# Attention, Mish FFN and four experts on one core: a new order for the first block, and expert weights fetched earlier

## The chip, the cores and the metric

The kernel runs as one program on one core of a Trainium2 chip. The metric is the device time of one execution in microseconds (us). The kernel before takes 945.83 us, the median of three runs (945.04, 945.83 and 948.88). What a measurement of this kernel can tell from no change is about 0.5%, some 4.7 us.

## The reference

Three stages are chained. Attention has 2 batches, 8 heads, 768 positions and 64 columns per head, with a bias that falls with distance; a key is kept when it is one of the first `n_global` (8) or among the last `n_local` (96). Its result, 1536 tokens of 512 columns, goes through a dense layer pair with a Mish gate, and that through four experts with ReLU, mixed by given probabilities:

```
scores = q @ k.T / 8 + bias;  a = softmax(where(keep, scores, -1e9));  x = a @ v
h = x @ w_in                       # 512 -> 2048
g = h * tanh(log1p(exp(min(h, 20))))
y = g @ w_out                      # 2048 -> 512
out = sum over e of p[e] * (relu(y @ w1[e]) @ w2[e])     # 512 -> 1024 -> 512
```

`w_in` and `w_out` come as 64-bit floats and are read as 64-bit words; everything else is 32-bit.

## The kernel before, in words

The 1536 tokens are three blocks of 512. For each block there are 16 pairs of attention (one pair: 128 queries and two heads), 16 steps of the FFN (128 hidden columns each) and 32 steps of the experts. A step is a "hidden" product, a gate, and a "project" product into four PSUM accumulators. The change touches block 0 alone, which is written out by hand in `first_block` (L788 to L886); blocks 1 and 2 are driven by the loop in `run` and are untouched.

In block 0 the products are single fp32 matmuls: `hidden_first` (L747) has four per step and `project_first` (L757) four per step, each shown by the trace as two instructions. The weights of FFN step c, 1 MB of 64-bit words, are loaded by `fetch` (L557) into one of four buffers (`big` 0 and 1, `raw` 0 and 1; table `TURN`), and turned into fp32 by `narrow` (L570): one ScalarE instruction (L584) and three VectorE instructions (L587, L589, L591), after which SyncE stores the result to HBM (L593, `wfirst`) for block 1. The buffer is free for step c+4 when step c is converted. All these loads and stores go through SyncE's one queue, in program order.

The order of the work in block 0 is a string, `PLAN` (L42). Each letter stands for one call, and the k-th use of a letter is for pair, step or part k. An engine executes its own instructions in exactly the order in which these calls issue them, so a letter that waits holds up everything behind it on the same engine. The letters:

- attention of one pair: S scores (PE), X bias and maximum (VectorE), E exponentials (ScalarE), D inverse sums of two pairs (VectorE), N scaling of the probabilities (GpSimd, L372), T transposes (PE), C copy of the transposes (ScalarE, L382) or Z the same on VectorE, A product with v (PE), F copy of the result of four pairs on ScalarE or G on VectorE (L396)
- conversion of one FFN step's weights: a (ScalarE), then t three times (VectorE)
- FFN: H hidden product, P project product (PE); the gate is e (ScalarE), c, n (VectorE), l (two on ScalarE), u, m, v, g (VectorE)
- w: a third of the splitting of an expert's weights into two parts (one ScalarE cast L609, two VectorE subtractions L612); i, j and 1 to 6: the start of block 1's attention

At H of step 0 all 16 pairs must be through (`n["F"] == 4`), since the FFN sums over all heads. Before the change the expert weights of steps 16 to 18 are fetched at the first `w`, from inside `part` (L852 to L861):

Of the kernel before, what the change touches and what calls it, by code (L numbers as in the profile page):

```python
# [11 lines left out]
I64 = mybir.dt.int64  # L12
AF = mybir.ActivationFunctionType
ALU = mybir.AluOpType

P = 128
B, H, S, D = 2, 8, 768, 64
# [7 lines left out]
NF1 = 16  # L25
# [14 lines left out]


PLAN = (  # L42
    "SSYXXESYSEXSEDXNXESNTDCTXSENANCTXESACTDEAXNSCNETXACTDEGANCSNaAXatTTtCSCAEXtAESDGNSXNTXEStTCDSEXNACNX"
    "EAtaTDTtNCSCANXEtAEtTTCGCADatNAaNtTtCTACtaAtGtHattteHacntlteHuamcvgnPetlctauHtmvngtlPteaucmHtvngtlPt"
    "eaucmHtvgntlPteaucmtHvngtlPteaucmtHvgntltPeucmtvHngtltPeucmtvHngtltaPeucmvngHtltautiPemcvgnPtltutHmw"
    "vwgwePwcnwlwHumvgePcnlHuwmwvwgeHcnlPuemcvngHlumvPegcnlPumvgj1P23456"
)

AFTER = {
# [8 lines left out]


@with_exitstack  # L60
def fused_attention_ffn_moe(ctx: ExitStack, tc: tile.TileContext, qkv, qk, vz, q_t, k_t, v_n, nloc, nglob, wff, wts, probs, out):
    nc = tc.nc
    nc.scalar.preload_act_table_set("natural_log_exp_and_others")
    const = ctx.enter_context(tc.tile_pool(name="const", bufs=1))


    nw = const.tile([P, 2], I64, tag="nw", name="nw")
    nc.sync.dma_start(nw[:, 0:1], nloc.unsqueeze(0).broadcast_to([P, 1]))
    nc.scalar.dma_start(nw[:, 1:2], nglob.unsqueeze(0).broadcast_to([P, 1]))

    early = ExitStack()
    setup = early.enter_context(tc.tile_pool(name="setup", bufs=1))
# [58 lines left out]
    big = [const.tile([P, 2048], F32, tag=f"big{n}", name=f"big{n}") for n in range(2)]  # L131
    for n, raw in enumerate(raws):
        at = slice(P if n < 2 else 0, 3 * P)
        nc.sync.dma_start(raw[:, 0:6 * P].rearrange("p (n c) -> p n c", n=2)[:, :, at],
                          qk[2 * n:2 * n + 2, :, at].rearrange("n p c -> p n c"))
        if wff.dtype == I64 and n % 2:
            nc.sync.dma_start(big[n // 2].bitcast(I64), wff[n // 2])

    narrow = nc.values_load(flag[0:1, 0:1], min_val=0, max_val=1)
    env = dict(qkv=qkv, qk=qk, vz=vz, q_t=q_t, k_t=k_t, v_n=v_n, wff=wff, wts=wts, out=out, ident=ident, nl=nl, ng=ng,  # L140
# [181 lines left out]
class FirstPair(NarrowPair):  # L322
# [43 lines left out]
        nc.vector.tensor_scalar(r, r, 1e-9, None, ALU.add)  # L366
        nc.vector.reciprocal(r, r)

    def scale(self):
        for j in range(2):  # L370
            p = self.p[:, j, 0:self.nk * P]
            self.nc.gpsimd.tensor_scalar(p, p, self.sum[:, j:j + 1], 0.0, ALU.mult, ALU.add)  # L372

    def trans(self):
        self.pt_ps = self.body.bank(f"pt{self.u}", 0)
# [147 lines left out]
class Body:  # L523
# [33 lines left out]
    def fetch(self, s):  # L557

        kind, t, n = self.steps[s]
        if kind == "ffn" and self.wide and t == 0:  # L560
            self.w64[s] = (self.big + self.twice)[TURN[n]].bitcast(I64)
            if n > 1 or not self.loaded:
                self.nc.sync.dma_start(self.w64[s], self.wff[n])
            return
        if kind == "ffn" and self.wide and t > self.first:
            return
        self.w32[s] = self.wpool.tile([P, 1024], F32, tag="w", name=f"w{s}")
        self.nc.sync.dma_start(self.w32[s], (self.wts if kind == "moe" else self.wfirst if self.wide else self.wff)[n])
# [219 lines left out]
    def first_block(self, ready, now):  # L788


        nc = self.nc
        pairs = [FirstPair(self, k) for k in range(TB // P * NP)]
        then = Attention(self, self.pair, 1)
        n = dict.fromkeys("SXEDNTCAFHecnlumvgPatw", 0)
        narrowing = [self.narrow(c) for c in range(NF1)]
        parts = [self.part(c) for c in range(NF1, NF1 + 3)]
        self.x0 = self.xy.tile([P, KC, TB], F32, tag="xyh", name="x0")

        for pair in pairs:
            pair.load()  # L800

        def ahead():
            while ready["fetch"] < NF1:
                c = ready["fetch"]
                before = [m for m in range(c) if TURN[m] == TURN[c]][-1:]
                if n["S"] < FREE.get(TURN[c], 0) or any(n["t"] < 3 * m + 3 for m in before):
                    break
                now("fetch", c + 1)

        def scores(k):  # L810
            pairs[k].scores()
            ahead()

        def warm(k):

            nc.tensor.matmul(self.bank(f"warm{k}", 0), self.ident, self.ident.unsqueeze(1).to_broadcast([P, 4, P]), start=True, stop=True)

        def inverse(k):
            assert n["E"] >= 2 * k + 2
            pairs[2 * k].inverse()  # L820

        def scale(k):
            assert n["D"] > k // 2
            pairs[k].scale()

        def take(engine):
            def run(k):
                assert n["A"] >= 4 * k + 4
                pairs[4 * k].take(engine)
                ahead()  # L830
            return run

        def hidden(s):
            assert n["F"] == 4 and n["t"] >= 3 * s + 3
            self.accumulating = True
            self.hidden_first(s)
            ahead()

        def project(s):
            self.project_first(s)  # L840

        def begin(c):
            assert (c < 2 or n["A"] >= min(2 * c - 2, len(pairs))) and (c < 10 or n["P"] > c - 10)
            next(narrowing[c])

        def convert(k):
            c = k // 3
            assert n["a"] > c
            next(narrowing[c], None)
            ahead()  # L850

        def part(k):  # L852
            c, third = divmod(k, 3)
            assert ready["fetch"] >= NF1 and n["S"] == len(pairs) and n["P"] >= 8 + 2 * c
            if third == 0:
                now("fetch", NF1 + 3)
                next(parts[c])
            try:
                parts[c].send("vector" if third else None)
            except StopIteration:  # L860
                pass  # L861

        def begin_next(k):
            assert n["t"] >= 36
            then.load(4)

        pair = lambda stage, *args: lambda k: getattr(pairs[k], stage)(*args)
        ops = {
            "S": scores, "X": pair("biased"), "E": pair("exps"), "D": inverse, "N": scale, "T": pair("trans"),
            "C": pair("copy", nc.scalar.copy), "Z": pair("copy", nc.vector.tensor_copy), "A": pair("av"),  # L870
            "F": take(nc.scalar.copy), "G": take(nc.vector.tensor_copy), "a": begin, "t": convert, "w": part,
            "Y": warm, "H": hidden, "e": self.mish_exp, "c": self.mish_cap, "n": self.mish_n, "l": self.mish_r,
            "u": self.mish_u, "m": self.mish_m, "v": self.mish_v, "g": self.gate_first, "P": project,
            "i": begin_next, "j": lambda k: then.split(k + 1),
            "1": lambda k: then.ahead(), "2": lambda k: then.scores(), "3": lambda k: then.softmax(),
            "4": lambda k: then.norm(), "5": lambda k: then.trans(), "6": lambda k: then.av(),
        }
        same = dict(Z="C", G="F")
        for token in PLAN:
            kind = same.get(token, token)  # L880
            for other in AFTER.get(kind, ()):
                assert n[other] > n[kind], (token, n[kind], other)
            ops[token](n.setdefault(kind, 0))
            n[kind] += 1
        ready["narrow"], ready["part"] = NF1, NF1 + n["w"] // 3
        return then, n["P"]  # L886
# [163 lines left out]
```

## Time and profile before

| | us |
|---|---|
| median of three runs | 945.83 |
| lowest, highest | 945.04, 948.88 |
| the profiled execution, its own time | 944.16 |
| its span, first to last instruction | 942.3 |
| TensorE (PE) busy in the span | 910.1 (97%) |
| VectorE, ScalarE, GpSimd busy | 527.8, 440.5, 379.6 |

The profiled execution is 1.67 us below the median. TensorE is busy nearly all the time; what can be won lies in its idle 32 us and in stretches where its clock is granted at half. A position in the trace is given in us from the span's start.

### The profile page before, as it was taken

How to read it: one execution, taken by the hardware profiler on the slowest of the kernel's cores; microseconds unless marked ns; L12 is line 12 of the kernel's file. 1: busy time of each engine (PE TensorE's matmuls, PEld its weight loads, DVE VectorE, ACT ScalarE, POOL GpSimd, SP SyncE). 2: the span in 40 equal slices, each digit the busy share in tenths (PEclk: the TensorE clock that was granted, in tenths of full speed). 3: DMA queues.
4: the chain of work that ended last, by engine and by line, in shares of the span. 5: the costliest groups of instructions: out<-in, count | busy, mean ns of one | idle time of the engine just before them, and what ended most of it. 6: DMA issues, size and time to landing. Idle time of an engine off the chain costs nothing.

```text
span 942.3 us, 11540 instructions
## 1 busy us (share of the span) xinstructions
PE 910.1 (97%) x3962; PEld 697.8 (74%) x3962; DVE 527.8 (56%) x1041; ACT 440.5 (47%) x860; POOL 379.6 (40%) x391
## 2 busy tenths in 40 slices
PE   8899979999899999999999999999999999999997
PEld 4744434787678888877777888888888888888886
DVE  4889957777673178888777621228886121112122
ACT  4844324776663256556776642323445332432330
POOL 3500000577575444437666754400004454454450
PEclk7999999999999999999999999999999999999999
DMA  8876450543312478863435223044562342323301
GB/s 308 296 284 224 160 196 1 201 157 134 112 68 90 156 263 298 296 261 134 143 126 201 69 90 106 29 178 179 195 252 94 107 134 99 103 90 97 105 23 49
DMA packets 40517, 143.88 MB, mean 153 GB/s; under 512 B 4736, under 2 KB 7552, under 8 KB 38400
## 3 DMA queue, kind: packets, MB, share of 16 engines
q1 hardware_dynamic: 40160, 143.02, 42.6%
q8 instruction: 33, 0.54, 0.2%
q14 instruction: 36, 0.29, 0.1%
q10 hardware_dynamic: 288, 0.03, 0.0%
HBM read 114.71 MB, written 28.31 MB: 152 GB/s over the span
## 4 chain that ended last, share of the span: by engine, by line
PE 71%; DVE 15%; ACT 8%; issue 2%; DMA 2%; POOL 0%; SPq 0%; ACTq 0%; DVEq 0%
PE h L627 29%; PE acc L733 28%; PE acc L762 5%; PE h L750 4%; DVE kl L231 2%; ACT p L275 1%; DVE nr L672 1%; PE o L297 1%; ACT wh L609 1%; DVE e L667 1%; PE pt L192 1%; DVE nr L678 1%; DVE n L655 1%; DVE e L682 1%; DVE n L648 1%
## 5 line engine op out<-in xcount | busy, mean ns | idle before, releaser
L612 POOL TENSOR_TENSOR wl<-w,wh 128x512 fp32r<-128x512 f32 x218 | 290.2, 1352 | 324.2 <-ACT wh L609 314.6
L708 DVE SCALAR_TENSOR_TENSOR gl<-h,gh 128x512 fp32r<-128x512 f32 x96 | 66.2, 689 | 267.3 <-ACT gh L703 267.3
L609 ACT CAST wh<-w 128x1024 fp32r<-128x1024 f32 x112 | 117.7, 1050 | 121.8 <-PE acc L733 106.2
L733 PE MATMUL acc<-wh,gh 128*128 128x512 f32 (+1 forms) x384 | 151.4, 394 | 0.0
L733 PE MATMUL acc<-wh,gl 128*128 128x512 f32 (+1 forms) x384 | 148.9, 388 | 0.0
L733 PE MATMUL acc<-wl,gh 128*128 128x512 f32 (+1 forms) x384 | 148.7, 387 | 0.0
L703 ACT ACTIVATE gh<-h 128x512 fp32r<-128x512 f32 x96 | 57.3, 597 | 114.4 <-PE h L627 114.4
L733 PEld LDWEIGHTS acc<-wh,gl 128*128 128x128 f32 x384 | 72.1, 188 | 15.1
L733 PEld LDWEIGHTS acc<-wl,gh 128*128 128x128 f32 x384 | 72.2, 188 | 14.1
L733 PEld LDWEIGHTS acc<-wh,gh 128*128 128x128 f32 x384 | 72.2, 188 | 14.0
L240 POOL TENSOR_TENSOR v<-raw,v 128x256 fp32r<-128x256 f32 x32 | 26.9, 841 | 116.6 <-ACT v L239 116.6
L750 PE MATMUL h<-x,w 128*128 128x512 f32 x128 | 57.2, 593 | 0.8 <-DVE x L396 0.8
L187 POOL TENSOR_SCALAR p<-p,st 128x256 f32<-128x256 f32 (+1 forms) x64 | 29.9, 479 | 66.5 <-DVE st L185 65.6
L627 PE MATMUL h<-y0h,wh 128*128 128x512 f32 x128 | 52.6, 411 | 2.5 <-DVE st L264 1.5
L275 ACT ACTIVATE p<-t,st 128x256 f32<-128x256 f32 (+1 forms) x96 | 46.4, 486 | 17.5 <-DVE st L264 16.5
L627 PE MATMUL h<-y1h,wh 128*128 128x512 f32 x128 | 50.7, 396 | 0.1
L627 PE MATMUL h<-y0h,wl 128*128 128x512 f32 x128 | 50.5, 395 | 0.0
L627 PE MATMUL h<-y0l,wh 128*128 128x512 f32 x128 | 50.4, 394 | 0.0
L627 PE MATMUL h<-y1l,wh 128*128 128x512 f32 x128 | 49.9, 390 | 0.0
L733 PE MATMUL acc<-gh,wh 128*128 128x512 f32 x128 | 49.9, 390 | 0.0
L627 PE MATMUL h<-y1h,wl 128*128 128x512 f32 x128 | 49.9, 390 | 0.0
L627 PE MATMUL h<-y2h,wh 128*128 128x512 f32 x128 | 49.9, 390 | 0.0
(152 smaller groups left out, 1821.3 us busy)
## 6 DMA issues: line engine op xcount, KB each, us to landing
w<-in_wts SPq DMA_DIRECT2D x96, 512.0 KB, 3.5
raw<-in_qkv SPq DMA_DIRECT2D x32, 512.0 KB, 3.9
big<-in_wff SPq DMA_DIRECT2D x10, 1024.0 KB, 5.9
wfirst<-w SPq DMA_DIRECT2D x16, 512.0 KB, 3.0
w<-wfirst SPq DMA_DIRECT2D x16, 512.0 KB, 4.2
wkeep<-wh SPq DMA_DIRECT2D x16, 512.0 KB, 3.1
wkeep<-wl SPq DMA_DIRECT2D x16, 512.0 KB, 2.9
wh<-wkeep SPq DMA_DIRECT2D x16, 512.0 KB, 3.2
```

The lines of the kernel that those rows point to most:

```text
L187: nc.gpsimd.tensor_scalar(self.p[:, j, 0:self.nk * P], self.p[:, j, 0:self.nk * P], st[:, 2 + j:3 + j], 0.0, ALU.mult, ALU.add)
L231: nc.vector.tensor_tensor(self.kl, self.k, self.kh.bitcast(F32), ALU.subtract)
L240: nc.gpsimd.tensor_tensor(vv[:, :, 1:3, :], v, vv.bitcast(F32)[:, :, 0:4:3, :], ALU.subtract)
L275: nc.scalar.activation(p[:, j, 0:n], t[:, j, 0:n], AF.Exp, bias=self.least[:, j:j + 1], scale=-1.0, accum_out=self.sum[:, j:j + 1])
L609: (nc.vector.tensor_copy if copy == "vector" else nc.scalar.copy)(hi, w)
L612: getattr(nc, engine or "gpsimd").tensor_tensor(lo[:, c], w[:, c], hi.bitcast(F32)[:, c], ALU.subtract)
L627: nc.tensor.matmul(ps, a[:, c], r[:, kc, :], start=m == 0, stop=m == 3 * KC - 1)
L703: self.nc.scalar.activation(gh, self.h[s], AF.Relu)
L708: nc.vector.scalar_tensor_tensor(gl, h, 0.0, gh.bitcast(F32), ALU.max, ALU.subtract)
L733: nc.tensor.matmul(acc[:, h], a, r, start=f == 0 and m == 0, stop=f == per - 1 and m == 2)
L750: self.nc.tensor.matmul(ps, self.w32[s][:, kc * P:(kc + 1) * P], self.x0[:, kc, :], start=kc == 0, stop=kc == KC - 1)
L762: self.nc.tensor.matmul(acc, w[:, 512 + d * P:512 + (d + 1) * P], g, start=s == 0, stop=s == NF1 - 1)
```

## The change

1. `PLAN` is another string of the same length. Up to the first H the counts of letters differ so: N 16 to 10, and V 0 to 6 (a new letter: the same scaling on VectorE); C 16 to 8 and Z 0 to 8; G 4 to 0 and F 0 to 4; a 6 to 5 and t 14 to 7. Over the whole string a, t, H, P, w and the gate's letters are as many as before, so 41 of 48 t stand behind the first H, where 34 stood.
2. The expert weights of steps 16 to 18 are fetched at H of step 0, and no longer at the first `w`.
3. The 64-bit weights of FFN step 1 are loaded behind all of block 0's attention inputs; before, they were loaded ahead of them.
4. `n_local` and `n_global` come in one load of one tensor on SyncE's queue; before, in two loads, on SyncE's and ScalarE's.

```
 PLAN = (
...
-    "eaucmHtvgntlPteaucmtHvngtlPteaucmtHvngtltPeucmtvHngtltPeucmtvHngtltaPeucmvngHtltautiPemcvgnPtltutHmw"
+    "tltumtPevcgnatHlttutPemcvagnHtltuatPemcvngtHltuatPemcvgntlHtutmPetvcgntlHtutmPetvcgnHtlaumtPevcgntlH"
...
-    nc.sync.dma_start(nw[:, 0:1], nloc.unsqueeze(0).broadcast_to([P, 1]))
-    nc.scalar.dma_start(nw[:, 1:2], nglob.unsqueeze(0).broadcast_to([P, 1]))
+    nc.sync.dma_start(nw, nums.unsqueeze(0).broadcast_to([P, 2]))
...
-        if wff.dtype == I64 and n % 2:
-            nc.sync.dma_start(big[n // 2].bitcast(I64), wff[n // 2])
+    if wff.dtype == I64:
+        nc.sync.dma_start(big[0].bitcast(I64), wff[0])
...
-    def scale(self):
+    def scale(self, engine):
         for j in range(2):
             p = self.p[:, j, 0:self.nk * P]
-            self.nc.gpsimd.tensor_scalar(p, p, self.sum[:, j:j + 1], 0.0, ALU.mult, ALU.add)
+            engine.tensor_scalar(p, p, self.sum[:, j:j + 1], 0.0, ALU.mult, ALU.add)
...
             self.w64[s] = (self.big + self.twice)[TURN[n]].bitcast(I64)
-            if n > 1 or not self.loaded:
+            if n > 0 or not self.loaded:
                 self.nc.sync.dma_start(self.w64[s], self.wff[n])
...
         def hidden(s):
+            if s == 0:
+                for c in range(NF1, NF1 + 3):
+                    self.fetch(c)
             assert n["F"] == 4 and n["t"] >= 3 * s + 3
...
             if third == 0:
-                now("fetch", NF1 + 3)
+                ready["fetch"] = NF1 + 3
                 next(parts[c])
...
-            "S": scores, "X": pair("biased"), "E": pair("exps"), "D": inverse, "N": scale, "T": pair("trans"),
+            "S": scores, "X": pair("biased"), "E": pair("exps"), "D": inverse, "N": scale(nc.gpsimd), "V": scale(nc.vector), "T": pair("trans"),
```

How the order moves, at three places. First VectorE at the end of block 0's attention (p3_2 and p3_3 are the probabilities of pairs 14 and 15, pt their transposes, w2, w3, w4 converted weights of those FFN steps, x0 the attention's result). Before:

```order
L396 COPY x0_179<-o2_0_491 128x4x128
L366 TENSOR_SCALAR st3_2_502<-st3_2_502 128x4
L367 RECIPROCAL st3_2_502<-st3_2_502 128x4
L591 SCALAR_TENSOR_TENSOR w2_512<-raw0_127,w2_512 128x1024
L587 TENSOR_SCALAR w3_581<-w3_581 128x1024
L589 SCALAR_TENSOR_TENSOR w3_581<-raw1_128,w3_581 128x1024
L591 SCALAR_TENSOR_TENSOR w3_581<-raw1_128,w3_581 128x1024
L587 TENSOR_SCALAR w4_591<-w4_591 128x1024
L396 COPY x0_179<-o3_0_574 128x4x128
```

And of the change:

```order
L381 COPY pt3_1_564<-pt3_1_555 128x512
L365 TENSOR_SCALAR st3_2_526<-st3_2_526 128x4
L366 RECIPROCAL st3_2_526<-st3_2_526 128x4
L371 TENSOR_SCALAR p3_2_524<-p3_2_524,st3_2_526 128x256 x2
L371 TENSOR_SCALAR p3_3_551<-p3_3_551,st3_2_526 128x256 x2
L586 TENSOR_SCALAR w1_453<-w1_453 128x1024
L381 COPY pt3_3_598<-pt3_3_589 128x512
L588 SCALAR_TENSOR_TENSOR w1_453<-big1_129,w1_453 128x1024
L590 SCALAR_TENSOR_TENSOR w1_453<-big1_129,w1_453 128x1024
```

The last two pairs are scaled by VectorE itself, right behind the inverses; five conversion instructions that stood between the inverses and the last copy are gone from there, and the conversions have reached step 1 or 2 where they had reached step 4.

Second, SyncE's queue where the expert weights (w16 to w18) are loaded. Before, behind the last stores of converted weights:

```order
L593 DMA wfirst_172<-w14_891 128x1024
L220 DMA raw0_127<-in_qkv 128x1024 x2
L220 DMA raw1_128<-in_qkv 128x1024 x2
L593 DMA wfirst_172<-w15_919 128x1024
L568 DMA w16_961<-in_wts 128x1024
L568 DMA w17_963<-in_wts 128x1024
L568 DMA w18_965<-in_wts 128x1024
```

And of the change, between the loads for FFN steps 5 (into big1) and 6 (into raw0):

```order
L592 DMA wfirst_170<-w1_453 128x1024
L562 DMA big1_129<-in_wff 128x1024
L567 DMA w16_614<-in_wts 128x1024
L567 DMA w17_616<-in_wts 128x1024
L567 DMA w18_618<-in_wts 128x1024
L592 DMA wfirst_170<-w2_477 128x1024
L562 DMA raw0_126<-in_wff 128x1024
L592 DMA wfirst_170<-w3_571 128x1024
L562 DMA raw1_127<-in_wff 128x1024
```

Third, ScalarE at the first FFN steps (e0, e1, e2 and r0, r1 belong to the gates of steps 0 to 2, w5 to w9 to conversions). Before:

```order
L584 ACTIVATE w6_633<-raw0_127 128x1024
L643 ACTIVATE e0_640<-h0_628 128x512
L584 ACTIVATE w7_649<-raw1_128 128x1024
L662 ACTIVATE r0_641<-n0_642 128x512
L663 ACTIVATE r0_641<-r0_641 128x512
L643 ACTIVATE e1_659<-h1_644 128x512
L584 ACTIVATE w8_669<-big0_129 128x1024
L643 ACTIVATE e2_686<-h2_663 128x512
L662 ACTIVATE r1_660<-n1_661 128x512
L663 ACTIVATE r1_660<-r1_660 128x512
```

And of the change:

```order
L642 ACTIVATE e0_630<-h0_620 128x512
L583 ACTIVATE w5_641<-big1_129 128x1024
L661 ACTIVATE r0_631<-n0_632 128x512
L662 ACTIVATE r0_631<-r0_631 128x512
L642 ACTIVATE e1_655<-h1_634 128x512
L583 ACTIVATE w6_660<-raw0_126 128x1024
L642 ACTIVATE e2_667<-h2_648 128x512
L661 ACTIVATE r1_656<-n1_657 128x512
L662 ACTIVATE r1_656<-r1_656 128x512
L583 ACTIVATE w7_685<-raw1_127 128x1024
```

The conversions stand at the same places between the gates, but for weights two steps nearer to their use: step 6 where step 8 stood, and its load stands behind the three expert loads.

## Rows read from the trace of the kernel before

**Rows 1.** Head of the page: the span.

```profile
span 942.3 us, 11540 instructions
```

**Rows 2.** Windows of block 0: length, busy us per engine (instructions), PEclk, DMA share, GB/s.

```profile
10.50:37.00 26.50, 26.35 (x160) 17.58 (x158) 18.26 (x83) 20.96 (x70) 10.19 (x24) 0.85 0.93 350
37.00:49.20 12.20, 9.02 (x69) 7.61 (x68) 10.50 (x17) 8.42 (x18) 8.11 (x8) 1.00 0.83 293
49.20:61.20 12.00, 10.57 (x25) 4.51 (x25) 10.08 (x14) 4.94 (x7) 0.00 (x0) 1.00 0.93 326
61.20:126.50 65.30, 65.30 (x152) 28.68 (x152) 62.06 (x87) 26.02 (x37) 0.00 (x0) 1.00 0.60 217
126.50:136.80 10.30, 5.35 (x10) 2.42 (x10) 6.25 (x11) 3.73 (x5) 0.00 (x0) 0.83 0.36 140
136.80:167.50 30.70, 30.70 (x74) 13.52 (x72) 19.99 (x34) 12.06 (x21) 0.73 (x1) 1.00 0.06 21
```

**Rows 3.** Chain of waits around the late stall: start us, us, what.

```profile
123.70 5.43 DMA w<-in_wts
...
157.40 10.31 PE acc L762 x24
```

**Rows 4.** Timeline of PE: start, us, instruction, idle before it and releaser.

```profile
49.23 10.57 PE L750 MATMUL h<-x,w 128*128 128x512 f32 x24 [0.79 <-DVE x L396]
61.20 3.67 PE L762 MATMUL acc<-gh,w 128*128 128x512 f32 x8 [1.40 <-DVE gh L682]
...
131.63 5.17 PE L762 MATMUL acc<-gh,w 128*128 128x512 f32 x8 [4.95 <-DVE gh L682]
```

**Rows 5.** Timeline of VectorE, the same gate instruction of two successive steps.

```profile
76.64 0.68 DVE L667 SCALAR_TENSOR_TENSOR e<-n,r 128x512 f32<-128x512 f32 x1
...
83.11 0.69 DVE L667 SCALAR_TENSOR_TENSOR e<-n,r 128x512 f32<-128x512 f32 x1
```

**Rows 6.** Timeline of GpSimd and PE, end of the attention: start, us, instruction.

```profile
33.71 1.84 POOL L372 TENSOR_SCALAR p<-p,st 128x256 f32<-128x256 f32 x4 [1.02 <-PE pt L192]
...
37.02 0.70 PE L355 MATMUL s<-qk 64*128 64x256 f32 x4
...
41.87 4.09 POOL L372 TENSOR_SCALAR p<-p,st 128x256 f32<-128x256 f32 x4 [0.74 <-PE pt L192]
```

**Rows 7.** Groups by line and form, 0 to 170 us: busy us, mean ns.

```profile
L589 DVE SCALAR_TENSOR_TENSOR w<-big,w 128x1024 int32<-128x1024 int32 x10 | 12.5, 1252 | 0.1
L587 DVE TENSOR_SCALAR w<-w 128x1024 int32<-128x1024 int32 x16 | 11.1, 692 | 0.7 <-ACT w L584 0.7
L643 ACT ACTIVATE e<-h 128x512 f32<-128x512 f32 x16 | 9.5, 592 | 17.0 <-PE h L750 16.9
L396 DVE COPY x<-o 128x512 f32<-128x512 f32 x4 | 2.7, 672 | 0.9 <-PE o L391 0.9
L115 DVE TENSOR_SCALAR dist<-rel,nlg 128x256 f32<-128x256 f32 x1 | 0.3, 333 | 0.0
```

**Rows 8.** FFN weight loads issued at 38.5 and 56.3; timeline of a waiting conversion.

```profile
L563 SPq DMA_DIRECT2D big<-in_wff x1: 386/386/386, 38.5 to 38.5; - x1
...
DMA to landing us min/median/max: 5.6/5.6/5.6
...
L563 SPq DMA_DIRECT2D big<-in_wff x1: 385/385/385, 56.3 to 56.3; - x1
...
DMA to landing us min/median/max: 8.6/8.6/8.6
...
55.73 1.16 ACT L584 ACTIVATE w<-raw 128x1024 f32<-128x1024 f32 x1 [2.17 <-DMA raw<-in_wff]
```

**Rows 9.** DMA issues: count, KB each, us to landing (expert loads in 123.6 to 126).

```profile
w<-in_wts SPq DMA_DIRECT2D x3, 512.0 KB, 6.3
...
nw<-in_nloc SPq DMA_DIRECT2D x1, 1.0 KB, 4.8
nw<-in_nglob ACTq DMA_DIRECT2D x1, 1.0 KB, 5.5
```

## What the change will do to the time

> **What bounds the kernel now.** I read the windows first, then the chain of waits, then the timelines of PE, of the other engines and the loads at the two ends of PE's idle stretches. The windows show where anything can be won [rows 2]: from 61.2 to 126.5 us PE is busy 65.30 of 65.30 us at full clock, from 136.8 to 167.5 likewise; the attention before 49.2 and the stretch from 126.5 to 136.8 (5.35 us busy of 10.30, granted clock 0.83) have the idle time that the change can reach. Blocks 1 and 2 come after 167.7 and keep their instructions and order; I let them shift as a whole. So the question is when block 0 ends: 157.40 + 10.31 = 167.71 us now [rows 3].
>
> Block 0's FFN is 16 hidden and 16 project products of 3.43 us each (10.31 us for three [rows 3]), 32 x 3.43 = 109.8 us. It starts at 49.23. Of the 118.5 us that it takes, 109.8 are products, 1.40 a wait of the first project product for its gate, 4.95 the wait before 131.63, and 5.17 - 3.43 = 1.74 the half-clock product behind it [rows 4]; 0.6 are small gaps. The 4.95 us end with VectorE, but the chain leads from there to the expert load issued at 123.70, 5.43 us to landing [rows 3]: the cast stands ahead of the gate's exponential on ScalarE, and both waited.
>
> **The change part by part.**
>
> *One load of the two numbers.* VectorE's first use waits for the later of two loads, 5.5 us on ScalarE's queue against 4.8 on SyncE's [rows 9]. One on SyncE's should land as that did: 0.7 us earlier. Bounds 0 and 0.7; I take 0.7, and all of the attention starts so much earlier.
>
> *The end of the attention.* From the last pair's scores to the first hidden product it is 49.23 - 37.02 = 12.2 us [rows 4, 6]. Behind its inverses GpSimd scales the last two pairs in 4.09 us, where the same work took 1.84 us at 33.71 [rows 6]; VectorE was converting weights meanwhile. The change puts these four scalings on VectorE; the trace has no such instruction, the nearest is another scalar instruction of 128x256 with 0.333 us [rows 7], so 4 x 0.333 = 1.33 us, from 0.7 (by the slope between that row and the 0.692 of 1024 columns) to 2.0. That saves 4.09 - 1.33 = 2.8 us. Two conversion instructions and a copy (0.69 + 1.25 + 0.67 = 2.6 us [rows 7]) also leave the place ahead of the last inverses; exponentials cover part of them, I count 1.4 us. The tail becomes 12.2 - 4.2 = 8.0 us.
>
> *Up to the last scores.* VectorE loses three conversion instructions (3.2 us) and two copies (1.3 us), gains six copies (at most 4.0 us) and four scalings (1.3 us): 0.8 us more. ScalarE loses about six copies and gains two. Following PE, VectorE and ScalarE down their new order with the trace's durations, I get the last scores at 38.6 us where they were at 37.02, since the copies now queue behind the maxima on VectorE. The bounds are 36.3 (the earlier start alone) and 39.8. With 8.0 us behind it the FFN starts at 46.6 (44.3 to 47.8), 2.6 us earlier.
>
> *The expert load.* All three land long before the `w` tokens, which now stand from step 13's products on; 4.95 + 1.74 = 6.7 us go. What is late next there: nothing that I see. VectorE's period for one step of gate and conversion is 83.11 - 76.64 = 6.47 us [rows 5], PE's 6.87. The 41 conversion instructions left at the FFN's start (34 before) cost 7 x 1.0 = 7 us more of VectorE, in 110 us of which it can spare 16 x 0.4 = 6.4 and what it idled at the old stall. So VectorE is tight but not the bound.
>
> *What the early load pushes back.* The three expert loads stand in SyncE's queue behind the load for FFN step 5 and ahead of that for step 6. Count time from the FFN's start. The load for step 5 can be issued when step 1 is converted, at about 0.5, and lands 5.6 us later (a load with an idle queue [rows 8]), at 6.1. Then come 1.57 MB of experts, and a store and a load of 1.57 MB for step 6. At 326 GB/s, what the queues moved from 49.2 to 61.2 with a DMA share of 0.93 [rows 2], step 6 lands at 6.1 + 4.8 + 4.8 = 15.7; at 350 GB/s it is 15.1. Its conversion on ScalarE is due at about 8 and stands ahead of the exponential and the logarithm of the gates of steps 2 and 1. So ScalarE stands, and the second project product with it. In the old order 61.20 - 55.73 = 5.47 us lay between the start of a waiting conversion and the product that hung on it [rows 4, 8]; here one exponential (0.59) and two conversion instructions (1.25 + 0.69) stand between them besides [rows 7], 8.0 us in all: the second project product starts at 23.1 to 23.7. The first starts at about 12.0, as before (61.20 - 49.23), because step 5's conversion waits as step 7's does now. Two products later PE is ready, at 18.9. The new stall is 4.2 to 4.8 us; I take 4.1, with a little rest for loads that run faster without stores. Between no wait at all and a landing 2.9 us later still (8.6 instead of 5.6 [rows 8]) it could be 0 to 7.
>
> [...]
>
> A stall of 4.95 us brought the granted clock to 0.83 in its window and a product to 5.17 us [rows 2, 4]; the 1.40 us stall did not (3.67). For one between them I take half of the loss, 0.9 us. [...]
>
> **The sum.** Block 0 ends at 46.6 + 109.8 + 1.7 (first project product) + 4.1 + 0.9 + 0.6 = 163.7 us, 4.0 before 167.7. The later load of step 1's weights and the copies moved off ScalarE I cost at nothing beyond the walk above: step 1 is wanted some 10 us after the third of these loads can be in. The profiled execution's own time of 944.16 us (span 942.3 [rows 1]) becomes 940.1. It stands 1.67 us under the median of 945.83, so on the scale of the runs I predict 945.83 - 4.0 = 941.8 us.
>
> **Rivals.**
>
> *The queue takes the expert loads in its stride.* For it: DMA share is only 0.60 from 61.2 on [rows 2], and step 6's weights could be asked for earlier if VectorE is ahead. Against it: the 1.57 MB stand in one queue, and conversions waited 2.17 us at 55.73 with less in the way [rows 8]. Then the new stall and its clock go and the old first wait stays: 4.0 + 4.1 + 0.9 = 9.0 us, 936.8 us.
>
> *It gives back what it takes.* The attention's end is bound by the longer copy queue on VectorE (start at 47.8), and the stall is at the upper end with the clock (7 + 1.7): block 0 ends at 47.8 + 109.8 + 1.7 + 7 + 1.7 + 0.6 = 168.6: 946.7 us, no change that can be told.
>
> *Slower: conversions only one step ahead of their use.* Where the old order had begun ten steps' conversions at step 3's hidden product, the new one has begun eight; every later conversion waits for a load issued some 6 us before. At 5.6 us to landing that holds, with ScalarE waiting a few tenths; from about 7.1 us on, the wait reaches PE at each of the loads for steps 8 to 13. At 8.6 us each [rows 8] it is 6 x (8.6 - 7.1) = 9 us, less the 4.0 gained: 950.8 us. For it: three loads in a row took over 8 us around 50. Against it: those had the backlog of the attention's end, and the share of 0.60 later.
>
> *It does not do what it says:* the `w` part could wait elsewhere, if the cast waits for ring buffers of weights. The windows give no sign; I leave it inside the second rival.
>
> **How the numbers follow.** The forecast has 0.45, the unhindered queue 0.30, give-back 0.14, slower 0.11. What can be told from no change here is 0.5%, 4.7 us, so that the forecast's 4.0 lies inside "no change" and nearly on its edge; of its 0.45 I give 0.17 to faster. Faster is 0.30 + 0.17 = 0.47; within 0.5% is 0.28 + 0.14 = 0.42; slower 0.11. The forecast's own range is 939 to 944.5. The range reaches from an unhindered queue with the FFN starting at 45 (935.0) to give-back (946.7), so 935.0 to 946.7 us.
>
> **What would show it.** In the changed kernel's profile: the first hidden product at 46 to 47; no expert load in the chain around 125, and full clock there; the second project product some 23 us after the first hidden product, behind a ScalarE conversion that waits for a load of FFN weights 6 to 8 us; block 0's last product ending near 163.7. A second project product 19 us after the start means the first rival. Several waits of PE behind conversions from step 8 on mean the slower one. A start of the FFN after 48 would show that my walk through the attention failed.

## The result, and the profile after

The changed kernel takes 938.00 us, the median of five runs (936.61 to 940.27), against 945.83 for five runs of the kernel before. The ratio is 0.991, with a 95% interval of 0.9883 to 0.9937: faster by 0.9%, more than the 0.5% that can be told here. The prediction was 941.8 (935.0 to 946.7). The profiled execution has a span of 936.2 us, 6.1 under the 942.3 of [rows 1].

First the windows of block 0 after the change, for comparison with [rows 2] (length, busy us per engine and instructions, granted clock, DMA share, GB/s):

```profile
10.50:37.00 26.50, 24.39 (x182) 18.72 (x181) 20.34 (x83) 21.14 (x67) 8.35 (x20) 1.00 0.92 340
37.00:49.20 12.20, 11.32 (x55) 7.31 (x55) 11.39 (x19) 4.56 (x9) 0.00 (x0) 1.00 0.45 159
49.20:61.20 12.00, 9.64 (x19) 3.93 (x18) 6.08 (x10) 5.40 (x8) 0.00 (x0) 0.86 0.94 360
...
126.50:136.80 10.30, 10.30 (x25) 4.56 (x25) 10.05 (x15) 3.55 (x5) 0.00 (x0) 1.00 0.76 268
```

The last row shows that the late stall is gone: PE is busy 10.30 us of 10.30 at full clock, where it had 5.35. The third shows what came in its place: between 49.2 and 61.2 PE now stands more (9.64 busy instead of 10.57), and the granted clock is 0.86 where it was 1.00. The idle time moved from the end of block 0 to its start.

The chain of waits names the load behind it (start us, us, what; to set beside [rows 3]):

```profile
46.55 12.00 DMA raw<-in_wff
...
66.57 5.40 PE acc L761 x8
...
150.94 10.31 PE acc L761 x24
```

The load of 1 MB issued at 46.55 is that for FFN step 6; it takes 12.00 us to land, where the load issued at 38.5 in the kernel before, with only a store of 0.52 MB just ahead of it in the queue, took 5.6 [rows 8]. Block 0 ends at 150.94 + 10.31 = 161.25, 6.46 us before the 167.71 of the kernel before. SyncE's timeline shows what the load stood behind:

```profile
43.44 0.37 SPq L562 DMA_DIRECT2D big<-in_wff  x1
43.91 1.98 SPq L567 DMA_DIRECT2D w<-in_wts  x3
46.13 0.33 SPq L592 DMA_DIRECT2D wfirst<-w  x1
46.55 0.40 SPq L562 DMA_DIRECT2D raw<-in_wff  x1
```

These are the load for step 5, three expert loads, a store, and the load for step 6. ScalarE pays (timeline; in brackets the idle time before and its releaser):

```profile
49.63 1.18 ACT L583 ACTIVATE w<-big 128x1024 f32<-128x1024 f32 x1 [2.50 <-DMA big<-in_wff]
...
58.58 1.12 ACT L583 ACTIVATE w<-raw 128x1024 f32<-128x1024 f32 x1 [6.10 <-DMA raw<-in_wff]
```

And PE's timeline, to set beside [rows 4 and 6]:

```profile
34.71 0.70 PE L354 MATMUL s<-qk 64*128 64x256 f32 x4
...
42.80 10.57 PE L749 MATMUL h<-x,w 128*128 128x512 f32 x24 [0.68 <-ACT x L395]
55.72 5.37 PE L761 MATMUL acc<-gh,w 128*128 128x512 f32 x8 [2.36 <-DVE gh L681]
...
66.57 5.40 PE L761 MATMUL acc<-gl,w 128*128 128x512 f32 x8 [2.05 <-DVE gl L681]
```

The last scores stand at 34.71 (before 37.02), the first hidden product at 42.80 (before 49.23): the FFN starts 6.43 us earlier. It then takes 161.25 - 42.80 = 118.45 us, as before (118.5). Its first two project products both wait (2.36 and 2.05 us) and run partly at half clock (granted clock 0.68 while each ran): 5.37 and 5.40 us instead of 3.43, which is 1.94 and 1.97 more. These 8.3 us are what the late stall, its clock and the old first wait cost (4.95 + 1.74 + 1.40 = 8.1 [rows 4]). So between these two profiles the whole gain is the attention's: what the FFN won at its end it lost at its start. How much of that loss is the expert load's and how much the new order's is asked in experiments 1, 2, 9 and 10.

In VectorE's timeline, the first use of the two numbers, the first softmax instruction, and the scaling of the last two pairs:

```profile
4.00 0.17 DVE L99 CAST words<-nw 128x4 f32<-128x4 int32 x1 [2.60 <-DMA nw<-in_nums]
...
8.21 0.27 DVE L263 CUSTOM_DVE_ANT_0 t<-s,bias 128x128 f32<-128x128 f32 x1
...
38.12 1.14 DVE L371 TENSOR_SCALAR p<-p,st 128x256 f32<-128x256 f32 x4
```

The scaling takes 1.14 us where GpSimd took 4.09 [rows 6]. The first softmax instruction stood at 10.57 before, so the start is 2.4 us earlier:

```profile
10.57 0.27 DVE L264 CUSTOM_DVE_ANT_0 t<-s,bias 128x128 f32<-128x128 f32 x1
```

The list of DMA issues gives the single load of the two numbers 3.2 us to landing, where the two had 4.8 and 5.5 [rows 9]:

```profile
nw<-in_nums SPq DMA_DIRECT2D x1, 2.0 KB, 3.2
```

The first of the windows holds one more difference: from 10.5 to 37 us the granted clock is 1.00 where it was 0.85 [rows 2]. PE's timeline shows where it begins, at the scores that wait for VectorE (it works on the two numbers there) and at the filler product (`warm`) behind them. Before:

```profile
8.81 1.23 PE L355 MATMUL s<-raw 64*128 64x128 f32 x8 [2.81 <-DVE dist L116]
9.97 2.07 PE L816 MATMUL warm<-ident 128*128 128x512 f32 x2
```

And after:

```profile
6.45 0.72 PE L354 MATMUL s<-raw 64*128 64x128 f32 x8 [0.27 <-DVE dist L115]
7.10 1.13 PE L815 MATMUL warm<-ident 128*128 128x512 f32 x2
```

Before, PE stood 2.81 us and then ran at half clock (granted 0.50 from 8.81 to 12.04 us); from 8 to 14 us the granted clock is 0.53 before and 1.00 after. In the four profiles with two loads (before, experiments 2, 4 and 10) a pair of filler products that started between 9.7 and 12 us took 2.07 us; in the ten with one (after and the other experiments) the pairs that started between 7 and 9.3 us took 1.12 or 1.13. Experiments 3 and 4 change the load alone. So the one load also kept the half clock away at the start of the attention.

### The profile page after: what moved, and what is told of

The parts are those of the page before. It is cut to its first block, busy times and chain, and to the rows that moved or that the text cites. A ratio compares the mean times of both kernels' runs of the same rounds, so it can differ in the third digit from the quotient of the medians.

```text
span 936.2 us, 11507 instructions
## 1 busy us (share of the span) xinstructions
PE 908.2 (97%) x3962; PEld 696.7 (74%) x3962; DVE 532.6 (57%) x1057; ACT 438.6 (47%) x856; POOL 369.6 (39%) x379
## 4 chain that ended last, share of the span: by engine, by line
PE 71%; DVE 14%; ACT 8%; DMA 3%; issue 3%; SPq 0%; ACTq 0%; POOL 0%; POOLq 0%; DVEq 0%
PE h L626 28%; PE acc L732 28%; PE acc L761 6%; PE h L749 4%; DMA raw<-in_wff 2%; DVE kl L230 2%; ACT p L274 2%; ACT wh L608 1%; DVE nr L671 1%; PE o L296 1%; DVE nr L677 1%; PE pt L191 1%; DVE n L654 1%; DVE e L681 1%; DVE e L666 1%
## 5 line engine op out<-in xcount | busy, mean ns | idle before, releaser
L732 PEld LDWEIGHTS acc<-wh,gl 128*128 128x128 f32 x384 | 72.1, 188 | 15.1
```

The costliest lines, as they stand in the source:

```text
L732: nc.tensor.matmul(acc[:, h], a, r, start=f == 0 and m == 0, stop=f == per - 1 and m == 2)
```

## The experiments

Each was timed beside the kernel before, whose median was 944.56 to 945.19 us. "After" is the changed kernel. The FFN's length is from the first hidden product to the end of the last project product of block 0.

**1. After, with the expert loads at step 8 of the FFN.**

```
-            if s == 0:
+            if s == 8:
                 for c in range(NF1, NF1 + 3):
                     self.fetch(c)
```

> The changed kernel, with one edit: the three expert loads are issued at the hidden product of step 8 and not of step 0. Theory A (in the changed kernel the expert loads delay the load of FFN step 6's weights: 12.0 us to landing, ScalarE waits 6.10 us for it, PE 2.05 us before the second project product, which then runs at half clock, 5.40 instead of 3.43): the load for step 6 lands in about 6 us, the second project product follows the third hidden product's successor without a stall, and some 4 us go: about 934.0. The stall before the first project product (2.36 us and its clock) stays. Rival B (the conversions are simply late, because only two of them are done before the FFN starts, whatever the expert loads do): ScalarE waits for step 6's weights almost as long, 937 to 938.5. Rival C: the loads at step 8 push back another FFN load and the stall comes there: 937 to 940.

Measured: 933.26 us, ratio 0.9873 (0.9857 to 0.9888). On PE's timeline:

```profile
44.48 10.57 PE L749 MATMUL h<-x,w 128*128 128x512 f32 x24 [0.68 <-ACT x L395]
57.19 5.37 PE L761 MATMUL acc<-gh,w 128*128 128x512 f32 x8 [2.14 <-DVE gh L681]
...
65.83 3.60 PE L761 MATMUL acc<-gl,w 128*128 128x512 f32 x8
```

The load for step 6 lands in 6.7 us instead of 12.00:

```profile
L562 SPq DMA_DIRECT2D raw<-in_wff x1: 383/383/383, 48.2 to 48.2; - x1
...
DMA to landing us min/median/max: 6.7/6.7/6.7
```

The second project product has no wait and full clock, and the FFN takes 114.2 us instead of 118.45. That is 4.2 us, and the second stall with its clock was 2.05 + 1.97 = 4.0. The late stall does not come back. The stall of step 1 is thus the price of placing the expert loads ahead of the load for step 6. The first stall and its clock (2.14 and 1.94 us) stay, so they are not the expert loads' doing. The result beats both kernels: all its runs (931.68 to 935.37) lie below all of after's.

**2. Before, with the expert loads at step 8.**

```
         def hidden(s):
+            if s == 8:
+                for c in range(NF1, NF1 + 3):
+                    self.fetch(c)
...
-                now("fetch", NF1 + 3)
+                ready["fetch"] = NF1 + 3
```

> The kernel before, with one edit: the three expert loads are issued at the hidden product of step 8, ahead of their use, and nothing else. Theory (the late stall of the kernel before, 4.95 us and a product at half clock, is the wait for these loads alone): both go, 6.7 us: about 939. Rival (the cast and subtraction of the experts' weights, or the last conversions, take the place of the wait): 942 to 945.8. If it lands at 939 the new order as a whole is worth no more than this one line.

Measured: 938.68 us, ratio 0.9928 (0.9915 to 0.9941). In the window 126.5 to 136.8 PE is busy throughout at full clock:

```profile
126.50:136.80 10.30, 10.30 (x25) 4.56 (x25) 7.02 (x12) 3.71 (x6) 0.00 (x0) 1.00 0.06 23
```

The FFN takes 114.3 us, 4.1 less than before. It is not the full 6.7 of the late stall, since the first project product now waits 2.51 us and takes 5.12, where it had 1.40 and 3.67 [rows 4]; why is not shown, since nothing ahead of it was changed. One moved call brings 6.5 us of the whole change's 7.8, without the new order.

**3. Before, with the two numbers in one load.**

```
-    nc.sync.dma_start(nw[:, 0:1], nloc.unsqueeze(0).broadcast_to([P, 1]))
-    nc.scalar.dma_start(nw[:, 1:2], nglob.unsqueeze(0).broadcast_to([P, 1]))
+    nc.sync.dma_start(nw, nums.unsqueeze(0).broadcast_to([P, 2]))
```

> The kernel before, with n_local and n_global in one load on SyncE's queue as in the change, and nothing else. In the two profiles the first softmax instruction of VectorE starts at 10.57 us before and 8.21 us after. Theory (the one load does it, since it lands 3.2 us after its issue instead of 5.5): 945.8 - 2.4 = 943.4. Rival 1 (only the difference of the two queues counts, 5.5 against 4.8 us): 945.1. Rival 2 (the start differs from one execution to the next and the load has no part in it): 945.8.

Measured: 944.89 us, ratio 0.9998 (0.9985 to 1.0011): no difference. The start did move, the first softmax instruction to 8.21 as in after, but PE then stood for its inputs:

```profile
20.80 0.70 PE L354 MATMUL s<-qk 64*128 64x256 f32 x4 [2.66 <-DMA qk<-in_qk]
...
49.69 10.57 PE L749 MATMUL h<-x,w 128*128 128x512 f32 x24 [0.78 <-DVE x L395]
```

In the old order the next load sets the pace, and 2.4 us won at the start are gone by the FFN.

**4. After, with the two loads of before** (the diff of experiment 3 the other way).

> The changed kernel, with n_local and n_global in two loads on two queues again, as before the change. Theory (the one load gives 2.4 us at the start): 938.0 + 2.4 = 940.4, first softmax instruction of VectorE at about 10.5 us. Rival 1: 938.7. Rival 2 (the load has no part in it): 938.0.

Measured: 940.01 us, ratio 0.995 (0.9931 to 0.9969). The last scores stand at 37.26 and the FFN starts at 45.34, 2.54 us later than in after:

```profile
37.26 0.70 PE L355 MATMUL s<-qk 64*128 64x256 f32 x4
...
45.34 10.57 PE L750 MATMUL h<-x,w 128*128 128x512 f32 x24 [0.68 <-ACT x L396]
58.77 5.37 PE L762 MATMUL acc<-gh,w 128*128 128x512 f32 x8 [2.86 <-DVE gh L682]
...
69.77 3.70 PE L762 MATMUL acc<-gl,w 128*128 128x512 f32 x8 [2.20 <-DVE gl L682]
```

The median is 2.0 us above after, but the intervals overlap, and the five profiles that share after's attention (after, experiments 1, 5, 11 and 12) start the FFN between 42.13 and 44.48. It points to some 2 us in the new order; it doesn't prove them.

**5. Experiment 1, with the gates of steps 0 and 1 ahead of conversions.**

```
-...FtHttteHtcantlHteuacmvnegclPtautmHtvngtlP...
+...FtHttteHcnlttaHeucmvngleactPtautmHtvngtlP...
```

> The kernel with the expert loads at step 8, with one more edit in PLAN: in the two steps after the first hidden products the gates of steps 0 and 1 stand ahead of the conversions of FFN weights 5 and 6 on ScalarE and VectorE (Htcantl Hteuacmvnegcl becomes Hcnltta Heucmvngleact). Theory (the stall that is left, 2.14 us before the first project product and 5.37 instead of 3.43 us for that product, is the gate of step 0 standing behind the conversion that waits for step 5's load): both go, 4.1 us, 933.3 - 4.1 = 929.2, the first project product some 10.6 us after the first hidden one and at full clock. Rival (the conversions are then too late for the hidden products of steps 3 to 5, and PE stalls there): 932 to 935.

Measured: 932.83 us, ratio 0.9867 (0.9846 to 0.9888); the theory's 929.2 failed, and the time is in the rival's range. PE:

```profile
42.13 10.57 PE L749 MATMUL h<-x,w 128*128 128x512 f32 x24 [0.68 <-ACT x L395]
53.65 3.67 PE L761 MATMUL acc<-gh,w 128*128 128x512 f32 x8 [0.96 <-DVE gh L681]
...
62.43 3.70 PE L761 MATMUL acc<-gl,w 128*128 128x512 f32 x8 [1.67 <-DVE gl L681]
```

The long wait became two short ones at full clock, yet the FFN still takes 114.2 us: what is not waited at the first project product is waited at the second (1.67 us) and at the last one (0.39 us, at 152.61). The rival had it at the hidden products, where the profile shows no such wait. That the late conversions set the pace whichever gate goes first is argued here; experiment 9, which does them earlier, supports it.

**6. Before, with one load of the numbers and step 1's weights loaded behind the attention's inputs.**

```
-        if wff.dtype == I64 and n % 2:
-            nc.sync.dma_start(big[n // 2].bitcast(I64), wff[n // 2])
+    if wff.dtype == I64:
+        nc.sync.dma_start(big[0].bitcast(I64), wff[0])
```

> The kernel before with its own PLAN, with the one load of n_local and n_global and with FFN step 1's weights loaded behind the attention's inputs, as in the change. The one load alone gave nothing (944.89 against 945.19), though VectorE started 2.4 us earlier; PE then waited 2.66 us for keys and queries. Theory (that megabyte stands ahead of the keys and queries in the queue, so an earlier start runs into the loads): now the start counts, 943.0, and the scores' wait for the load shrinks under 1 us. Rival (the old order's attention is bound by GpSimd and the conversions, not by the start): 944.5 to 945.5.

Measured: 948.79 us, ratio 1.0039 (1.0026 to 1.0052), slower than experiment 3 by 3.9 us. The theory fell: PE's keys and queries come earlier (a wait of 1.77 us that ends at 17.99, where it was 2.66 ending at 20.80), but ScalarE stands for step 1's weights, which the old order converts too soon for this load:

```profile
26.81 1.12 ACT L583 ACTIVATE w<-big 128x1024 f32<-128x1024 f32 x1 [4.33 <-DMA big<-in_wff]
```

**7. After, with the scaling back on GpSimd** (V becomes N at the six places).

> The changed kernel, with the last six pairs' probabilities scaled on GpSimd instead of VectorE (each V in PLAN an N), nothing else. Theory (the shorter tail of the attention, 8.1 us from the last scores to the first hidden product instead of 12.2, comes for the larger part from the scaling's place): the tail grows by 4.1 - 1.1 = 3 us where GpSimd shares its time with conversions, by 0.7 where it doesn't; there are three such pairs of pairs, so 1.5 to 4 us slower: 939.5 to 942. Rival (the tail is shorter only since the conversions left it): under 1 us, 938 to 939.

Measured: 939.91 us, ratio 0.9946 (0.9928 to 0.9964). GpSimd's timeline and PE's:

```profile
38.32 2.09 POOL L371 TENSOR_SCALAR p<-p,st 128x256 f32<-128x256 f32 x4 [1.97 <-DVE st L366]
```
```profile
43.63 10.57 PE L749 MATMUL h<-x,w 128*128 128x512 f32 x24 [0.68 <-ACT x L395]
```

GpSimd now needs 2.09 us for the last four scalings, not 4.09; the order leaves only one VectorE conversion instruction beside it (0.69 us in after). From the last scores (34.71) to the FFN it is 8.9 us against 8.1 in after: of the 4.1 us by which the tail shortened, the place of the scaling is worth 0.8. By the median this kernel is 1.9 us slower than after, by the profile's span (935.3) 0.9 faster; the times don't tell them apart.

**8. After, with step 1's weights loaded early again** (the diff of experiment 6 the other way).

> The changed kernel, with FFN step 1's weights loaded ahead of the attention's inputs again, nothing else. Theory (the megabyte delays keys and queries; PE waits 1.21 us for them in the changed kernel, 2.66 in the kernel before with one load): PE waits 2.5 to 3.5 us, the FFN starts 1.5 to 2.5 us later, 939.5 to 940.5. Rival (later waits in the attention swallow it): 938.

Measured: 939.63 us, ratio 0.9938 (0.992 to 0.9957). PE's timeline:

```profile
15.52 0.68 PE L390 MATMUL o<-pt,vz 128*128 128x128 f32 x4 [1.85 <-DMA vz<-in_vz]
...
20.88 0.70 PE L354 MATMUL s<-qk 64*128 64x256 f32 x4 [1.64 <-DMA qk<-in_qk]
```

With 0.60 us at 11.31 PE waits 4.1 us for its inputs, where after waits once, 1.21 us at 18.23. The FFN starts at 44.70, just beyond the 42.13 to 44.48 of the five profiles with after's attention. Time and start are as the theory said, but the median is 1.6 us above after with overlapping intervals: it points that way and is not settled.

**9. After, with the conversions back in the tail and scaling on GpSimd.**

```
-...ADVVTtTCaZAtAtFtHttte...
+...ADNNtttTTCaZAAFtHttte...
```

> The changed kernel with the end of its attention made like that of the kernel before: the last two pairs scaled on GpSimd, and three conversion instructions of VectorE beside them, between the inverses and the transposes (DVVTtTCaZAtAtFt becomes DNNtttTTCaZAAFt). GpSimd alone in that place cost little: 2.09 us for the two pairs against 4.09 in the kernel before, and 8.9 us of tail against 8.1. Theory D (the 4.09 us of the kernel before come from conversions that VectorE runs at the same time): the scaling takes 3.5 to 4.1 us, the tail is 10 to 11.5 us. Rival (GpSimd was slow there for another reason): 1.8 to 2.2 us, and the tail is 9 to 10 us, by the copies that wait behind the conversions. The time: the FFN starts 1.5 to 3 us later, but the load for FFN step 5 can be asked for before it starts, and up to 2.4 + 1.9 us of the stall at the first project product go, so 936 to 941 by either.

Measured: 934.37 us, ratio 0.989 (0.9872 to 0.9907), below the 936 to 941 expected. All its runs (933.78 to 934.92) lie below all of after's. The timelines of GpSimd, PE and SyncE:

```profile
37.74 4.02 POOL L371 TENSOR_SCALAR p<-p,st 128x256 f32<-128x256 f32 x4 [13.85 <-DVE st L366]
```
```profile
46.08 10.57 PE L749 MATMUL h<-x,w 128*128 128x512 f32 x24 [0.68 <-ACT x L395]
56.98 3.67 PE L761 MATMUL acc<-gh,w 128*128 128x512 f32 x8 [0.33 <-DVE gh L681]
...
63.92 3.60 PE L761 MATMUL acc<-gl,w 128*128 128x512 f32 x8
```
```profile
41.41 0.37 SPq L562 DMA_DIRECT2D big<-in_wff  x1
41.88 1.97 SPq L567 DMA_DIRECT2D w<-in_wts  x3
...
47.01 0.38 SPq L562 DMA_DIRECT2D raw<-in_wff  x1
```

And ScalarE's:

```profile
55.44 1.17 ACT L583 ACTIVATE w<-raw 128x1024 f32<-128x1024 f32 x1 [1.59 <-DMA raw<-in_wff]
```

The scaling takes 4.02 us again once three conversion instructions run beside it, and the tail is 46.08 - 34.18 = 11.9 us again. But the FFN takes only 110.7 us and ends at 156.8, in these profiles ahead of after (161.25) and of experiment 1 (158.7). With three conversion instructions done while PE waits for the scaling, step 5's load goes out 4.7 us before the FFN starts (in after 0.6 us behind the start), step 6's lands in 8.4 us, and ScalarE waits 1.6 us for it, not 6.1. Here the expert loads, still at step 0, cost next to nothing: the 32 products alone are 109.8 us. So the conversions' place decides more than the scaling's: by leaving the tail they moved their own work, and the loads behind it, into PE's first steps.

**10. Before, with the expert loads at step 0** (experiment 2 with `s == 0`).

> The kernel before with its own order, the expert loads at the hidden product of step 0 instead of step 8, where they gave 938.68. Theory A (1.57 MB in the queue at the FFN's start delay the next loads of FFN weights by some 4 to 5 us, whatever the order): the loads for steps 8 and 9, which are asked for at about 51 and 55 us, take 11 to 13 us to land instead of 8.5, the first project products stall 2 to 5 us and run at half clock: 941 to 945. Rival (the old order has converted four steps before the FFN starts and so has the slack for it): 938 to 940.

Measured: 939.63 us, ratio 0.9949 (0.9933 to 0.9964), 1 us above experiment 2 with overlapping intervals, and in the rival's range. The load behind the experts, in the view of one tile's instructions:

```profile
L563 SPq DMA_DIRECT2D big<-in_wff x1: 387/387/387, 51.0 to 51.0; - x1
...
DMA to landing us min/median/max: 12.6/12.6/12.6
```
```profile
61.07 5.37 PE L762 MATMUL acc<-gh,w 128*128 128x512 f32 x8 [2.26 <-DVE gh L682]
...
70.69 3.70 PE L762 MATMUL acc<-gl,w 128*128 128x512 f32 x8 [0.82 <-DVE gl L682]
```

The queue does the same (12.6 us, after 12.0), but the delayed loads are those for steps 8 and 9, with two steps more in hand: the second stall is 0.82 us at full clock, and the FFN takes 115.4. The first stall, 2.26 us, is as in experiment 2 (2.51), where no expert load stood ahead.

**11 and 12. Experiments 1 and 5, each load of FFN weights issued ahead of the store of the step whose conversion freed its buffer.** The store is made a step of its own in `narrow`, and `ahead` lets it go after the fetches:

```
         if self.first:
+            yield
             nc.sync.dma_start(self.wfirst[s], m)
...
+            while kept and n["t"] >= 3 * kept[0] + 3:
+                next(narrowing[kept.pop(0)], None)
```

> The kernel with the expert loads at step 8, with the load of each FFN step's weights issued ahead of the store of the converted weights that frees its buffer, instead of behind it. Theory (the stall left before the first project product, 2.14 us and 1.94 of half clock, is the wait for step 5's load, 2.30 us on ScalarE, and the store of 0.52 MB ahead of that load costs it 0.4 us of issue and 1.4 us of the queue): the load lands 1.5 to 1.8 us earlier, the stall is under 0.8 us and without half clock: 933.3 - 3.4 = 930. Rival (VectorE's conversions, not the load, are late there): 932.5 to 933.5.

> Load ahead of store, as in the other kernel of this call, and the gates of steps 0 and 1 ahead of the conversions, which alone gave 932.83: there the first stalls were 0.96 and 1.67 us, but the block's FFN took as long as without it, 114 us, since VectorE then ran from load to conversion to load. Theory (the loads' landing is what sets that pace): 1.5 us earlier at each load gives back 2 to 4 us, 929 to 931. Rival (VectorE's work itself sets it): 932 to 933.

Measured: 932.52 us (0.9877, 0.9854 to 0.9899) and 933.22 us (0.9883, 0.9864 to 0.9901): no gain over 933.26 and 932.83. The first project product of the first of them still waits:

```profile
55.85 5.37 PE L762 MATMUL acc<-gh,w 128*128 128x512 f32 x8 [1.89 <-DVE gh L682]
```

The store in front was hardly the limit: without it ScalarE still waited 2.02 us for step 5's load, until 6.36 us after the FFN's start; in experiment 1, behind it, 2.30 us, until 6.63. Experiments 1, 5, 11 and 12 lie between 932.5 and 933.3 and can't be told apart. Combining experiment 9's earlier conversions with scaling on VectorE and the loads at step 8 was not tried.

## Why the prediction was right or wrong

**The time.** 938.0 lies within the range, and the chance for faster came in, but between the forecast of 941.8 and the first rival's 936.8. It was not that rival's mechanism: the queue did not take the expert loads in its stride. The forecast's mechanism at the expert loads held. That the time fell inside the range is in part luck: by the profiles the FFN started 3.8 us before the forecast's 46.6, and then took 1.35 us more than the forecast's 117.1. The sum also had two small slips. It counts some 0.3 us of the first project product twice (by the same terms the kernel before would end block 0 at 168.0 instead of 167.71), and the lower end of the range works out at 935.2, not 935.0; neither matters for the outcome.

**One load of the two numbers: mis-sized.** The step said that one load "should land as that did: 0.7 us earlier". It landed in 3.2 us, and the first softmax instruction came 2.4 us earlier. In the old order this was worth nothing (experiment 3), because the next inputs were late. In the new one the last scores came 2.3 us earlier. With two loads they stand at 37.26 (experiment 4), in the five profiles of after's attention at 34.05 to 36.39; this makes it likely that most of the 2.3 is the load's, without settling it. The step also missed what else the later load cost: PE's stand of 2.81 us and the half clock behind it (granted 0.50).

**The last scores: the step that put the FFN's start outside its range.** I had them at 38.6 "since the copies now queue behind the maxima on VectorE", with 36.3 as the earliest; they stood at 34.71. Of the 3.9 us between, 1.7 are the first load's mis-size. The other 2.2 are the delay by copies that I had summed on VectorE (2.3 us over the 36.3) and that this pair of profiles does not show. Other profiles show a smaller one: experiment 4, whose first softmax instruction stands where before's does (10.60), has its last scores at 37.26, and three profiles of the old attention (before, experiments 2 and 10) at 37.02, 35.52 and 36.03, so 0.2 to 1.7 us. My walk also carried over durations from a stretch in which PE ran at half clock in part (granted 0.85 from 10.5 to 37 us [rows 2], after the change 1.00); what that difference is worth was not separated.

The FFN therefore started at 42.80, outside 44.3 to 47.8. Experiments 3, 4, 6 and 8 fit a gain that is tied together: the earlier start needs the inputs early, those need step 1's weights late, and those need the late conversions. Of the four, 3 (no gain) and 6 (a loss) can be told from noise, 4 and 8 cannot. The single shares are not settled, since profiles with the same attention differ by up to 2.35 us in where the FFN starts. The same holds for the whole: the FFN starts at 47.76, 48.25 and 49.23 in the three profiles of the old attention and at 42.13 to 44.48 in the five of the new, so the mean gain is 5.4 us, and 6.43 is that of one pair.

**The end of the attention: right in sum, half wrong in reason.** The tail was forecast at 8.0 us and is 8.09; the scaling at 1.33 and is 1.14. This share does not vary: 12.2 us in the three profiles of the old attention and 8.1 in the five of the new. But 2.8 of the gain was credited to the change of engine. On GpSimd with one conversion instruction beside it the scaling takes 2.09 us (experiment 7), with three 4.02 (experiment 9). The conversions' departure did most of it. Why conversions slow the scaling, the runs don't show.

**The expert load: right.** The late stall of 6.7 us went, in after and in experiments 1, 2 and 10.

**What the early load pushes back: right in mechanism, its parts mis-sized.** Step 6's weights landed at 46.55 + 12.00 - 42.80 = 15.75 us after the FFN's start (15.1 to 15.7 forecast). The second project product came at 66.57 - 42.80 = 23.8 (23.1 to 23.7). Its stall was 2.05 instead of 4.1, since PE was itself late: the first project product started at 12.9 instead of 12.0 and ran 1.94 us long, so PE was ready at 21.7 instead of 18.9. The first product's 0.9 us came from step 5's load, which ended ScalarE's wait 6.8 us after the FFN's start where before the wait for step 7's ended at 6.5, and from a chain of 6.1 us instead of 5.47 from there to the product. The forecast had taken this wait over from the kernel before as it was. Experiment 1 takes the second stall and its clock away by moving the loads alone; experiment 10 shows the same delay with other weights in its path. The measured 15.75 is what the rows' 326 GB/s gave (15.7), from parts that differ: ScalarE's wait for step 5's load ended at 6.8 and not at 6.1, and from 46 to 56 us the queues moved 373 GB/s.

**The clock: missed on the first stall.** I let the first wait pass at full clock and took half of 1.74 for the second. Both cost it whole, 1.94 and 1.97; of this some 0.25 us stand behind a stall at full clock too (3.67 to 3.70 instead of 3.43; granted 1.00 during the 3.67 of the kernel before). For stalls of about 2 us the runs don't give one answer, as the last section shows.

**The slower rival** asked for waits at each load from step 8 on. The trace shows none: from 66.57 on, the chain is PE without a gap to the end of block 0.

## What to carry to other kernels

A prefetch is not free because its own data is early: here 1.57 MB in SyncE's queue made the load behind them, 6.7 us to landing, into a 12.0 us one (experiment 1 against after). So ask which weights stand behind it and how far ahead of use they are. Moving that call by eight steps was worth 4.7 us by the medians in the new order and 1 us in the old one, whose loads had two steps more in hand. Work that is moved out of one critical tail may own the next load's start; follow it to the buffer that it frees before calling it gone.

## What the runs showed that I had not expected

- **Two small loads against one.** Two loads of 1 KB on two queues landed in 4.8 and 5.5 us, one of 2 KB in 3.2. The first use stands at 3.90 to 4.06 us with one load (after, experiments 1, 3 and 6) and at 6.37 to 6.42 with two (before, experiments 2 and 4).
- **Half clock without a sharp length.** Stalls of PE ahead of a project product of 0.33 to 1.68 us were followed by products at full clock (3.67 to 3.70). Stalls of 1.89, 2.04, 2.05, 2.14, 2.26, 2.29, 2.36, 2.51, 2.58, 2.63 and 2.86 us were followed by products of 5.1 to 5.4 us. But after 1.91 us in experiment 7 and 2.20 us in experiment 4 the product took 3.70. So a stall of 2.05 us cost 1.97 us more behind it in after and one of 2.20 only 0.27 in experiment 4: its length alone does not tell the two apart.
- **Conversions beside GpSimd.** GpSimd's four scalings took 1.84 us beside VectorE's softmax work (before, at 33.71) and 4.02 beside three conversion instructions (experiment 9), two of which themselves took 1.38 us instead of the 1.22 in after.
- **A varying start.** With the same compute instructions in the attention, five profiles started the FFN at 42.13 to 44.48 us, with waits for one input load of 0.34 to 2.18 us; behind the longest, in experiment 1, the next scores took 1.23 us where they took 0.70 in after, and the products with v 2.99 instead of 2.05. A comparison of single profiles says little below that.
